# A fused attention and mixture-of-experts kernel: its two hand-written step lists laid in another order

## The chip, the cores and the metric

The kernel runs on one core of a Trainium2 chip. The metric is the device time of one launch in microseconds (us). Engines are named as in the profile: PE (TensorE), PEld (its weight loads), DVE (VectorE), ACT (ScalarE), POOL (GpSimd) and SP, whose queue issues most DMAs.

## The reference

Attention with rotary embedding over 8 batches of 8 heads, 576 tokens, head size 64; its output, 4608 tokens of 512 values, goes to the one of 8 experts with the highest gate logit.

```python
q_rot, k_rot = rotate(q), rotate(k)
scores = scale * q_rot @ k_rot^T            # per batch and head, 576 x 576
attn = exp(scores - max) / (sum + 1e-9)
x = (attn @ v) as [4608, 512]               # heads side by side
expert = argmax(x @ w_gate);  g = softmax weight of that expert
out[token] = g * (relu(x[token] @ w1[expert]) @ w2[expert])
```

## The kernel before

**Two halves.** The attention handles 32 pairs of heads (4 pairs make a batch). The experts follow: tokens are gathered by expert into slots of 256, and each slot does two products (lines 1378 and 1514). The attention's output goes to DRAM (x_dram) batch by batch, and the positions of the tokens are scattered into per-expert lists in DRAM (xlist).

**Steps and their names.** The attention is cut into 2213 small steps. A step is written as a name whose last letter is its engine (p PE, v DVE, a ACT, g POOL, d SP's queue), with the number n of its pair. For a pair:

- FP loads q and k (1152 KB; two buffers, so pair n + 2 waits until pair n is rotated). RKm and RQm multiply by the rotation (POOL), RBb adds the two halves. HB rounds to the high part (ACT), LB makes the low part (POOL), and DX and DY (SP) copy these parts to the other half of the partitions; DW and DZ are small copies of the same kind.
- S0 to S8 are nine score products on PE (lines 760 and 771), each into a pair of PSUM banks; M0 to M8 take the row maxima (DVE), E0 to E8 the exponentials (ACT), which give the banks back.
- TA0, TA1, TB0, TB1 and TR turn the exponentials on PE (lines 798, 831, 835). The ten steps cA0x to cRy copy the results from PSUM to SBUF, on DVE or ACT (line 716); c3 is a small one for the rest rows.
- V0 and V1 are the long products with the values (line 870), V4 is that of the rest rows. U0 and U1 copy their results out, on DVE or ACT (line 897). O turns them back, X scales them into the rows of x (DVE).

Four PSUM pairs are handed round in the order in which the steps take and give them.

**The gate.** After each fourth pair the steps gL to gY find the expert of every token. gP counts on PE; gD, gQ, gO, gU and gY are small steps on POOL; gS stores the rows. gI0 to gI4 are the list scatters: five indirect DMAs a batch that POOL issues (line 1088). Their number is that of the batch's last pair, so gI3 with 23 belongs to batch 5. Those of the last two batches come after the lists.

**What sets the order.** FIRST and LAST name every attention step in the order in which it is emitted. chained_emit ties each instruction to the one before it on its engine, so each engine works in list order; an engine that waits holds up all that stands behind it. A third list, PLAN, gives the places that remain and is not changed.

**The seam.** LAST also holds steps that begin with m: mRI loads the lists of the first three slots (line 556; it needs the last scatter of batch 5), mGA and mGB gather rows of the first two slots (POOL, line 608), mXA and mXB turn them on PE (line 1326), mS.. and mZ.. split the weights in a high part (ACT) and a low part (DVE or POOL, line 1573), and mM1 is the first expert product.

```python
def listed_steps(steps):
    for tok, n in steps:
        if tok[0] == "m":
            chained_emit(lambda: tail[tok[1:-1]](tok[-1]), True)
        elif tok[0] == "g":
            gate_step(tok, n // NP, True)
        else:
            step(tok, n, True)
```

Of the kernel before, what the change touches and what calls it, by code (L numbers as in the profile page):

```python
# [31 lines left out]
    ("RQav", 0), ("RQcv", 0), ("RQbv", 0), ("FPd", 1), ("RKcv", 0), ("HQa", 0), ("RKav", 0), ("DWd", 0), ("DXd", 0),  # L32
    ("LQv", 0), ("RKbv", 0), ("HKa", 0), ("DYd", 0), ("RQcv", 1), ("S4p", 0), ("RQav", 1), ("LKv", 0), ("S3p", 0),
    ("S7p", 0), ("RQbv", 1), ("HQa", 1), ("RKcv", 1), ("M4v", 0), ("M3v", 0), ("E3a", 0), ("LQg", 1), ("FPd", 2),
# [10 lines left out]
    ("DYd", 2), ("M4v", 2), ("TRp", 1), ("E4a", 2), ("cRya", 1), ("cRxv", 1), ("DXd", 2), ("TA0p", 1), ("TB1p", 1),  # L45
# [7 lines left out]
    ("TRp", 2), ("E4a", 3), ("DYd", 3), ("S7p", 3), ("VPd", 2), ("CTd", 0), ("cRyv", 2), ("cA0xa", 2), ("RQmg", 5),  # L53
# [13 lines left out]
    ("TRp", 4), ("VPd", 4), ("FPd", 8), ("LBg", 6), ("VPd", 5), ("cB1xv", 4), ("cA0xv", 4), ("cRxv", 4), ("cA0ya", 4),  # L67
# [1689 lines left out]
```

## Time and profile before

| what | us |
|---|---|
| median of 3 runs (lowest, highest) | 922.22 (920.4, 926.88) |
| the profiled execution | 923.04 |
| its span, first to last instruction | 921.2 |
| PE busy in the span | 903.7 |
| start, up to the first score product | 13.7 |
| attention, 13.7 to 453.9 | 440.2 |
| experts, 453.9 to 921.2 | 467.3 |

The profile is of one execution. A busy PE is one with at least one product in flight; products overlap, so stretched ones count as busy as well.

### The profile page before, as it was taken

What the parts mean: (1) busy time and instruction counts of PE and PEld (TensorE: products, weight loads), DVE (VectorE), ACT (ScalarE), POOL (GpSimd) and SP (SyncE); (2) the same over time, 40 slices, a digit from 0 to 9 for tenths busy, and PEclk for the clock granted to TensorE, in tenths of its full rate; (3) what the DMA queues carried; (4) which work ended last, traced back from release to release, by engine and by line L of the source; (5) the groups of instructions that cost most, each with busy time, mean ns of one, the idle gap of its engine ahead of it and who ended that gap; (6) DMA issues with size and microseconds to landing.
All of it is one profiled execution on the core that took longest, in us unless ns stands there. A gap on an engine that the chain in (4) does not pass through costs nothing.

```text
span 921.2 us, 26711 instructions
## 1 busy us (share of the span) xinstructions
PE 903.7 (98%) x10101; PEld 730.9 (79%) x10101; DVE 748.4 (81%) x1361; ACT 629.1 (68%) x1190; POOL 640.8 (70%) x446
## 2 busy tenths in 40 slices
PE   8999999999999999999999999999999999999997
PEld 7666677677767766766799999999999999997786
DVE  6877788898988978788777677777777777778997
ACT  5888888778878888886645555555555555556886
POOL 3999787898998998894645566666666666664111
PEclk9999999999999999999999999999999999999999
DMA  8677565656674676535521577425426311165991
GB/s 284 185 208 225 158 170 182 216 161 181 198 218 127 184 217 195 158 76 169 204 90 38 146 236 240 125 67 161 125 60 194 97 49 49 44 195 203 406 339 52
DMA packets 71162, 152.73 MB, mean 166 GB/s; under 512 B 28601, under 2 KB 39673, under 8 KB 66032
## 3 DMA queue, kind: packets, MB, share of 16 engines
q1 hardware_dynamic: 61424, 130.69, 45.7%
q0 software_dynamic: 9600, 20.23, 7.0%
q8 instruction: 83, 1.36, 0.6%
q14 instruction: 55, 0.45, 0.2%
HBM read 161.32 MB, written 22.69 MB: 200 GB/s over the span
## 4 chain that ended last, share of the span: by engine, by line
PE 26%; issue 21%; POOL 18%; ACT 2%; POOLq 1%; DMA 1%; DVE 1%; DVEq 0%; ACTq 0%
PE pb L870 6%; POOL xg L589 6%; POOL xt L589 6%; PE pb L1378 5%; PE pb L771 5%; POOL out_dram L1404 4%; PE pb L1514 4%; PE pb L798 3%; POOL xsm L1256 1%; DMA out_dram<-y,gi 1%; PE pb L884 1%; POOLq L1447 1%; PE pb L920 1%; ACT PT L716 1%; ACT pn L787 1%
## 5 line engine op out<-in xcount | busy, mean ns | idle before, releaser
L776 DVE TENSOR_REDUCE negm<-pb 128x1 f32<-128x576 f32 x288 | 205.7, 749 | 45.0 <-PE pb L771 31.1
L787 ACT ACTIVATE pn<-pb,negm 128x576 f32<-128x576 f32 x256 | 188.2, 742 | 56.6 <-DVE negm L776 53.6
L1378 PE MATMUL pb<-xh,w1h 128*128 128x256 f32 x544 | 153.8, 283 | 0.0
L1378 PE MATMUL pb<-xh,w1l 128*128 128x256 f32 x544 | 153.7, 283 | 0.0
L1378 PE MATMUL pb<-xl,w1h 128*128 128x256 f32 x544 | 153.7, 283 | 0.0
L771 PE MATMUL pb<-rKQ 64*128 64x288 f32 x768 | 138.2, 312 | 2.6 <-ACT pn L787 1.0
L771 PE MATMUL pb<-rKQ,rX 64*128 64x288 f32 x768 | 138.4, 312 | 1.3 <-ACT PT L716 0.5
L870 PE MATMUL pb<-PT,vn 128*64 128x320 f32 (+1 forms) x1024 | 138.1, 412 | 0.1
L589 POOL DMA_INDIRECT xg<-x_dram,gp x64 | 91.4, 1428 | 54.6 <-DVE gp L399 38.1
L1282 DVE TENSOR_TENSOR w2l<-r,w2h 128x1024 fp32r<-128x1024 f32 x89 | 107.3, 1216 | 19.6 <-ACT w2h L1281 17.3
L771 PEld LDWEIGHTS pb<-rKQ,rX 64*128 64x128 f32 x768 | 107.5, 185 | 18.6 <-ACT pn L787 7.5
L771 PEld LDWEIGHTS pb<-rKQ 64*128 64x128 f32 x768 | 107.4, 185 | 18.3 <-ACT pn L787 11.1
L589 POOL DMA_INDIRECT xt<-x_dram,gp x56 | 80.4, 1436 | 49.2 <-DVE gp L399 31.7
L716 DVE COPY PT<-pb 128x512 f32<-128x512 f32 (+1 forms) x192 | 100.8, 564 | 11.2 <-PE pb L835 5.7
L870 PEld LDWEIGHTS pb<-PT,vn 128*64 128x64 f32 x1024 | 67.9, 136 | 51.2 <-issue 8.1
L1282 DVE TENSOR_TENSOR w1l<-r,w1h 128x1024 fp32r<-128x1024 f32 x88 | 104.6, 1219 | 2.7 <-ACT w1h L1281 2.2
L1378 PEld LDWEIGHTS pb<-xh,w1h 128*128 128x128 f32 x544 | 106.1, 195 | 0.6
L1378 PEld LDWEIGHTS pb<-xh,w1l 128*128 128x128 f32 x544 | 106.1, 195 | 0.5
L1514 PE MATMUL pb<-w2h,hh 128*128 128x512 f32 x272 | 106.2, 390 | 0.0
L1378 PEld LDWEIGHTS pb<-xl,w1h 128*128 128x128 f32 x544 | 106.1, 195 | 0.0
L1514 PE MATMUL pb<-w2l,hh 128*128 128x512 f32 x272 | 106.0, 390 | 0.0
L1514 PE MATMUL pb<-w2h,hl 128*128 128x512 f32 x272 | 105.9, 389 | 0.0
(224 smaller groups left out, 2014.5 us busy)
## 6 DMA issues: line engine op xcount, KB each, us to landing
r<-in_moe_w_dram SPq DMA_DIRECT2D x136, 512.0 KB
qk<-in_qk_dram SPq DMA_DIRECT2D x31, 1152.0 KB
r<-in_moe_w1q_dram SPq DMA_DIRECT2D x56, 512.0 KB
rX<-rKQ SPq DMA_DIRECT2D x128, 144.0 KB
x_dram<-xt SPq DMA_DIRECT2D x8, 1032.0 KB
vn<-in_v_dram SPq DMA_DIRECT2D x32, 256.0 KB
xlist<-mark SPq DMA_DIRECT2D x3, 408.0 KB
qk<-in_qk_dram SPq DMA_DIRECT2D x2, 576.0 KB
```

Of the source, the lines that this page charges most:

```text
L589: nc.gpsimd.indirect_dma_start(out=t[:, k], out_offset=None, in_=x_dram.rearrange("n (q w) -> (n q) w", q=4), in_offset=bass.IndirectOffse ...
L716: return (nc.scalar.copy if eng == "a" else nc.vector.tensor_copy)(out=o, in_=i).ins
L771: nc.tensor.matmul(sp[:, r, 0:HS], lhsT=(st["KQ"][rows[r], 1] if r == h else st["X"][rows[r]])[:, a, i * P:(i + 1) * P], rhs=parts(st["KQ" ...
L776: nc.vector.tensor_reduce(out=st["negm"][:, j:j + 1], in_=st["S", j][:, :, 0:HS], axis=AX.XY, op=ALU.max, negate=True)
L787: nc.scalar.activation(out=parts(pt), in_=sp[:, :, 0:HS], func=AF.Exp, bias=st["negm"][:, j:j + 1], scale=1.0, accum_out=z)
L798: nc.tensor.transpose(tp[:, r, k * 256 + i * 64:k * 256 + i * 64 + 64], pn[rows[r], i, c:c + P], ident[rows[r], rows[r]])
L870: m = nc.tensor.matmul(st["av"][rows[h ^ half], half, 0:w], lhsT=st["vn"][:, h, kt, :], rhs=st["PT"][:, 4 * h + kt, half * 256:half * 256 ...
L884: m = nc.tensor.matmul(st["av"][rows[h ^ a], a, 0:k * D].rearrange("p (i q) -> p i q", i=k), lhsT=vr[n % NVR][rows[h]], rhs=st["PT"][rows[ ...
L1282: nc.vector.tensor_tensor(out=lo, in0=src, in1=hi.bitcast(F32), op=ALU.subtract)
L1378: m = nc.tensor.matmul(hp[:, fi], lhsT=w, rhs=x, start=(i == 0), stop=(i == len(todo) - 1))
L1404: sc = nc.gpsimd.indirect_dma_start(out=out, out_offset=bass.IndirectOffsetOnAxis(ap=si[:, t:t + 1], axis=0), in_=y, in_offset=None, bound ...
L1514: m = nc.tensor.matmul(yp[:, t], lhsT=h[:, fi, ts_], rhs=w[:, fi], start=(g == 0 and fi == 0 and i == 0), stop=(g == FQ - 1 and fi == 1 an ...
```

## The change

FIRST and LAST are replaced. The new lists hold the same 2213 steps, FIRST 1862 of them and LAST 351 (before: 1845 and 368). Nearly all stand in another place, 90 on another engine: copies out of PSUM (cA0x to cRy) go 29 times from DVE to ACT and 25 times back, U0 and U1 18 times to ACT and 12 times to DVE, c3 three times each way, and mS1l goes from DVE to POOL. The list scatters gI stand at other places among the long products V0 and V1. PLAN and all functions stay. The diff, cut to places that the text speaks of:

```diff
--- before.py
+++ after.py
@@ -29,277 +29,276 @@
     ("gBv", 0), ("gGv", 3),
 ]
 FIRST = [
...
-    ("RQmg", 16), ("E0a", 13), ("S8p", 13), ("RZv", 11), ("M5v", 13), ("E5a", 13), ("Op", 10), ("RKmg", 16),
...
-    ("U0a", 11), ("HBa", 15), ("M2v", 13), ("M6v", 13), ("V1p", 11), ("DXd", 14), ("gYg", 7), ("gI3g", 3),
...
+    ("M6v", 12), ("S2p", 12), ("S1p", 12), ("E6a", 12), ("DXd", 13), ("V1p", 10), ("S4p", 13), ("M1v", 12),
+    ("RKmg", 16), ("HBa", 14), ("E1a", 12), ("TB0p", 12), ("M2v", 12), ("RZv", 11), ("E2a", 12), ("cB0ya", 12),
...
+    ("M6v", 14), ("M1v", 14), ("DXd", 15), ("RQmg", 17), ("S2p", 14), ("gLv", 11), ("gI3g", 3), ("HBa", 16),
...
-    ("V1p", 29), ("E7a", 31), ("E6a", 31), ("mRId", 0), ("U1v", 29), ("S8p", 31), ("mL10d", 0), ("gOg", 27),
-    ("S2p", 31), ("E5a", 31), ("S3p", 31), ("U0v", 29), ("M8v", 31), ("V0p", 30), ("M2v", 31), ("VPd", 31),
-    ("E8a", 31), ("TB1p", 31), ("E2a", 31), ("DZd", 31), ("gSd", 27), ("M3v", 31), ("E3a", 31), ("TRp", 31),
-    ("TB0p", 31), ("cB1ya", 31), ("cRya", 31), ("V4p", 30), ("cRxv", 31), ("cB1xv", 31), ("cB0xv", 31), ("cB0ya", 31),
-    ("Op", 29), ("TA0p", 31), ("mS0ha", 0), ("TA1p", 31), ("cA1ya", 31), ("cA0xv", 31), ("V1p", 30), ("U0a", 30),
-    ("mGAg", 0), ("mS0lg", 0), ("cA0yv", 31), ("cA1xa", 31), ("V0p", 31), ("mGBg", 0), ("gPp", 27), ("mS2ha", 0),
-    ("mS1ha", 0), ("RZv", 31), ("mS3ha", 0), ("Xv", 29), ("mCMx", 0), ("c3v", 31), ("mS1lv", 0), ("gRv", 27),
...
+    ("S8p", 31), ("E6a", 31), ("gOg", 27), ("M8v", 31), ("S2p", 31), ("U1a", 29), ("S3p", 31), ("V0p", 30),
+    ("mS3ha", 0), ("mL10d", 0), ("VPd", 31), ("E8a", 31), ("M2v", 31), ("gI3g", 23), ("M3v", 31), ("mS3lv", 0),
+    ("E2a", 31), ("TB1p", 31), ("E3a", 31), ("cB1yv", 31), ("TB0p", 31), ("cB0ya", 31), ("gSd", 27), ("TA0p", 31),
+    ("cB1xv", 31), ("cB0xa", 31), ("V4p", 30), ("TA1p", 31), ("cA0yv", 31), ("cA0xv", 31), ("mS2ha", 0), ("U0v", 30),
+    ("TRp", 31), ("cA1ya", 31), ("V1p", 30), ("cRxv", 31), ("mS0ha", 0), ("mRId", 0), ("DZd", 31), ("cRya", 31),
+    ("RZv", 30), ("cA1xv", 31), ("mGAg", 0), ("V0p", 31), ("mS0lg", 0), ("mCMx", 0), ("Op", 29), ("c3a", 31),
+    ("mXAp", 0), ("mGBg", 0), ("U1v", 30), ("mL20d", 0), ("V4p", 31), ("gPp", 27), ("mS1ha", 0), ("mX1ha", 0),
+    ("gRv", 27), ("mX0ha", 0), ("mL21d", 0), ("V1p", 31), ("mX1lv", 0), ("mL23d", 0), ("U0a", 31), ("mS2lg", 0),
+    ("mS1lg", 0), ("Op", 30), ("mL22d", 0), ("RZv", 31), ("gUg", 27), ("mZ0ha", 0), ("U1v", 31), ("mX0lv", 0),
+    ("gVv", 27), ("Op", 31), ("gYg", 27), ("mCRx", 0), ("mXBp", 0), ("Xv", 31), ("Xv", 29), ("mM1p", 0), ("Xv", 30),
+    ("mZ3ha", 0), ("mH1ha", 0), ("mH1lv", 0), ("mM0p", 0), ("mM2p", 0), ("mZ3lv", 0), ("mZ2ha", 0), ("mH0ha", 0),
+    ("mH2ha", 0), ("mZ1ha", 0), ("mZ0lg", 0), ("mM3p", 0), ("mZ2lv", 0), ("mY0ha", 0), ("mH0lv", 0), ("mH2lv", 0),
+    ("mN0p", 0), ("mY1ha", 0), ("mLBd", 0), ("mT2ha", 0), ("mT1ha", 0), ("mZ1lv", 0), ("mT0ha", 0), ("mY0lv", 0),
+    ("mY1lv", 0), ("mH3ha", 0), ("mT3ha", 0), ("mN1p", 0), ("mT2lv", 0), ("mN2p", 0), ("mT1lv", 0), ("mT0lv", 0),
+    ("mT3lv", 0), ("mH3lv", 0), ("mN3p", 0), ("mO1a", 0), ("mO0v", 0), ("mLCd", 0),
 ]
```

## Rows read from the trace of the kernel before

**Rows 1.** The page's first part: busy us (share of span) xinstructions by engine.
```profile
PE 903.7 (98%) x10101; PEld 730.9 (79%) x10101; DVE 748.4 (81%) x1361; ACT 629.1 (68%) x1190; POOL 640.8 (70%) x446
```

**Rows 2.** Windows: width, busy us (instructions) by engine, PE's granted clock, DMA share, GB/s.
```profile
13.70:80.00 66.30, 61.31 (x968) 43.78 (x966) 53.60 (x91) 57.86 (x138) 61.05 (x25) 1.00 0.73 216
80.00:200.00 120.00, 118.92 (x1943) 84.07 (x1942) 100.01 (x194) 99.53 (x235) 101.64 (x57) 1.00 0.63 188
200.00:320.00 120.00, 119.40 (x1984) 84.86 (x1982) 107.69 (x214) 94.66 (x222) 110.12 (x64) 1.00 0.60 177
320.00:453.90 133.90, 132.04 (x2184) 92.08 (x2184) 107.39 (x213) 106.87 (x249) 105.47 (x96) 1.00 0.56 168
453.90:921.20 467.30, 459.40 (x2842) 413.56 (x2842) 372.06 (x641) 264.51 (x341) 260.90 (x192) 1.00 0.45 147
```

**Rows 3.** The chain that ended last, in mid-span: start us, us, what.
```profile
287.02 2.30 PE pb L870 x16
300.20 2.31 PE pb L870 x16
```

**Rows 4.** Waits before 454 us: engine, tile <- releaser: us in total, times, longest.
```profile
PEld pb L771 <- ACT pn L787: 18.6, 48, 0.6
POOL qk L710 <- DMA qk<-in_qk_dram: 1.8, 2, 1.0
```

**Rows 5.** Copies of DVE and ACT before 460 us: busy us, mean ns.
```profile
L716 DVE COPY PT<-pb 128x512 f32<-128x512 f32 x144 | 90.4, 680 | 10.6 <-PE pb L835 5.7 <-PE pb L798 4.6 <-ACT pn L787 0.2
L716 ACT COPY PT<-pb 128x512 f32<-128x512 f32 x176 | 93.2, 605 | 7.2 <-PE pb L798 5.9 <-PE pb L835 0.6
```

**Rows 6.** Groups of POOL before 454 us, the list scatters.
```profile
L1088 POOL DMA_INDIRECT xlist<-tid,lpi x30 | 30.6, 1019 | 7.2 <-issue 6.1 <-POOL y L705 0.2
```

**Rows 7.** Timeline of DVE and POOL at 264 us, of DVE at 304 us.
```profile
263.58 3.07 DVE L716 COPY PT<-pb 128x512 f32<-128x512 f32 x5
...
265.74 1.01 POOL L1088 DMA_INDIRECT xlist<-tid,lpi  x1 [0.16 <-issue]
...
303.96 3.07 DVE L716 COPY PT<-pb 128x512 f32<-128x512 f32 x5
```

**Rows 8.** Timeline of SP's queue and of POOL at 330 to 340 us.
```profile
330.05 5.20 SPq L665 DMA_DIRECT2D qk<-in_qk_dram  x2
...
337.30 2.65 POOL L710 TENSOR_TENSOR qk<-qk,rotk 128x1152 f32<-128x1152 f32 x1 [0.98 <-DMA qk<-in_qk_dram]
```

**Rows 9.** Timeline of POOL, SP's queue and PE from 425 to 455 us.
```profile
425.77 1.06 POOL L1088 DMA_INDIRECT xlist<-tid,lpi  x1 [0.46 <-issue]
435.38 0.25 POOL L1058 TENSOR_TENSOR de<-eq,bs 128x40 f32<-128x40 f32 x1 [8.55 <-DVE bs L1055]
436.57 1.15 POOL L608 DMA_INDIRECT xg<-x_dram,gi  x1 [0.54 <-issue]
438.03 1.00 POOL L608 DMA_INDIRECT xg<-x_dram,gi  x1 [0.30 <-issue]
...
431.17 2.73 SPq L556 DMA_DIRECT2D gi<-xlist  x3
...
449.08 0.85 PEld L1326 LDWEIGHTS pb<-cst,xg 128*128 128x128 f32 x8 [0.49 <-issue]
...
454.68 0.37 PE L1378 MATMUL pb<-xh,w1h 128*128 128x256 f32 x1
```

**Rows 10.** DMA issues: out<-in queue xcount, KB each or us to landing.
```profile
x_dram<-xt SPq DMA_DIRECT2D x8, 1032.0 KB
xg<-x_dram,gi POOLq DMA_INDIRECT x4, 5.3
```

**Rows 11.** Timeline of DVE and POOL at 447 to 453 us.
```profile
447.40 1.23 DVE L1573 TENSOR_TENSOR w1l<-r,w1h 128x1024 fp32r<-128x1024 f32 x1 [0.94 <-ACT w1h L716]
449.37 3.29 DVE L1573 TENSOR_TENSOR w1l<-r,w1h 128x1024 fp32r<-128x1024 f32 x1
...
449.22 2.36 POOL L1573 TENSOR_TENSOR w1l<-r,w1h 128x1024 fp32r<-128x1024 f32 x1
```

More of the change, by code (lines that the diff above doesn't have):

```diff
@@ L31 @@
 FIRST = [
-    ("RQav", 0), ("RQcv", 0), ("RQbv", 0), ("FPd", 1), ("RKcv", 0), ("HQa", 0), ("RKav", 0), ("DWd", 0), ("DXd", 0),
-    ("LQv", 0), ("RKbv", 0), ("HKa", 0), ("DYd", 0), ("RQcv", 1), ("S4p", 0), ("RQav", 1), ("LKv", 0), ("S3p", 0),
-    ("S7p", 0), ("RQbv", 1), ("HQa", 1), ("RKcv", 1), ("M4v", 0), ("M3v", 0), ("E3a", 0), ("LQg", 1), ("FPd", 2),
[10 rows of a table removed]
-    ("DYd", 2), ("M4v", 2), ("TRp", 1), ("E4a", 2), ("cRya", 1), ("cRxv", 1), ("DXd", 2), ("TA0p", 1), ("TB1p", 1),
[7 rows of a table removed]
-    ("TRp", 2), ("E4a", 3), ("DYd", 3), ("S7p", 3), ("VPd", 2), ("CTd", 0), ("cRyv", 2), ("cA0xa", 2), ("RQmg", 5),
[13 rows of a table removed]
@@ L67 @@
-    ("TRp", 4), ("VPd", 4), ("FPd", 8), ("LBg", 6), ("VPd", 5), ("cB1xv", 4), ("cA0xv", 4), ("cRxv", 4), ("cA0ya", 4),
[28 rows of a table removed]
-    ("U0v", 6), ("cA1ya", 8), ("Xv", 5), ("gVv", 3), ("TRp", 8), ("S4p", 9), ("RZv", 7), ("cRxa", 8), ("RKmg", 11),
[7 rows of a table removed]
-    ("cA1ya", 9), ("TRp", 9), ("cB1xa", 9), ("DZd", 9), ("DWd", 11), ("E4a", 10), ("RQmg", 12), ("gSd", 3),
[5 rows of a table removed]
-    ("V4p", 8), ("U0v", 8), ("RZv", 8), ("V1p", 8), ("S4p", 11), ("LBg", 11), ("DYd", 11), ("DZd", 10), ("HBa", 12),
[26 rows of a table removed]
-    ("FPd", 17), ("DYd", 14), ("DWd", 15), ("LBg", 15), ("cA1yv", 13), ("cA0xa", 13), ("cRxa", 13), ("TB1p", 13),
[4 rows of a table removed]
@@ L142 @@
-    ("DXd", 15), ("M2v", 14), ("HBa", 16), ("RQmg", 17), ("E2a", 14), ("DYd", 15), ("V1p", 12), ("gMv", 11),
[8 rows of a table removed]
-    ("S1p", 15), ("M1v", 15), ("RQmg", 18), ("HBa", 17), ("RKmg", 18), ("DXd", 16), ("gVv", 11), ("RZv", 13),
[4 rows of a table removed]
-    ("cB1yv", 15), ("S7p", 16), ("FPd", 19), ("DWd", 18), ("M0v", 16), ("DYd", 17), ("gEa", 11), ("DXd", 17),
[14 rows of a table removed]
-    ("RBbg", 20), ("LBg", 19), ("DWd", 19), ("FPd", 22), ("cRxa", 17), ("gI4g", 3), ("cRyv", 17), ("cA0xv", 17),
[56 rows of a table removed]
-    ("E7a", 24), ("DYd", 25), ("U1a", 22), ("gYg", 19), ("TA1p", 24), ("TRp", 24), ("DZd", 24), ("DXd", 25),
[16 rows of a table removed]
@@ L245 @@
-    ("cB0ya", 26), ("DWd", 28), ("cB1yv", 26), ("cB1xa", 26), ("cRxv", 26), ("FPd", 30), ("RBbg", 29), ("cRya", 26),
[3 rows of a table removed]
-    ("gMv", 23), ("c3v", 26), ("gDg", 23), ("DZd", 26), ("DXd", 28), ("M8v", 27), ("S7p", 27), ("gQg", 23),
[4 rows of a table removed]
+    ("FPd", 1), ("RQav", 0), ("RQcv", 0), ("RQbv", 0), ("RKcv", 0), ("RKav", 0), ("HQa", 0), ("LQv", 0), ("RKbv", 0),
+    ("RQav", 1), ("RQcv", 1), ("HKa", 0), ("LKv", 0), ("RQbv", 1), ("DWd", 0), ("RKcv", 1), ("S4p", 0), ("DXd", 0),
[49 rows of a table added]
+    ("RQmg", 9), ("cA1xa", 6), ("cRya", 6), ("cRxv", 6), ("S7p", 7), ("DWd", 8), ("E8a", 7), ("cB1yv", 6), ("VPd", 6),
[20 rows of a table added]
@@ new lines @@
+    ("cA1ya", 9), ("RKmg", 13), ("RBbg", 12), ("cB1xa", 9), ("E4a", 10), ("TRp", 9), ("cRxa", 9), ("cRyv", 9),
[28 rows of a table added]
+    ("M2v", 13), ("V1p", 11), ("gYg", 3), ("DYd", 14), ("gWv", 7), ("M6v", 13), ("gYg", 7), ("E2a", 13), ("DWd", 14),
[10 rows of a table added]
+    ("cB0yv", 14), ("LBg", 16), ("E4a", 15), ("gBv", 11), ("DZd", 14), ("DYd", 15), ("cB1xa", 14), ("gOg", 11),
[7 rows of a table added]
+    ("S4p", 16), ("RKmg", 18), ("cB0xa", 15), ("VPd", 14), ("LBg", 17), ("RQmg", 18), ("RZv", 14), ("RZv", 15),
[29 rows of a table added]
+    ("gQg", 15), ("DZd", 18), ("E0a", 19), ("gBv", 15), ("DWd", 21), ("M5v", 19), ("E5a", 19), ("gOg", 15),
[11 rows of a table added]
@@ L254 @@
+    ("VPd", 19), ("cB1yv", 20), ("gVv", 15), ("TRp", 20), ("RQmg", 23), ("cB1xa", 20), ("cRya", 20), ("cRxa", 20),
[3 rows of a table added]
+    ("M7v", 21), ("DWd", 22), ("gGv", 15), ("RZv", 20), ("M5v", 21), ("E7a", 21), ("FPd", 25), ("RQmg", 24),
[57 rows of a table added]
 ]
 LAST = [
[46 rows of a table removed]
-    ("mLCd", 0),
[33 rows of a table added]
+    ("TRp", 31), ("cA1ya", 31), ("V1p", 30), ("cRxv", 31), ("mS0ha", 0), ("mRId", 0), ("DZd", 31), ("cRya", 31),
[10 rows of a table added]
 ]
```

482 rows, old and new, of tables (FIRST, LAST) are left out of this document.

## The prediction

> **What bounds the kernel now.** I read the stages first, then TensorE's pace inside one of them, then the waits, and last the hand-over between the two halves. The page says that PE is busy for 903.7 us, 98% of the span [rows 1]; that alone could hide stretched instructions, so the windows come next [rows 2]. They cut the span into the start (13.7 us, up to the first score product), the attention (13.7 to 453.9) and the experts (467.3). In all of their rows the granted clock is 1.00, that is 2.4 GHz. In the attention PE has nothing in flight for 66.30 - 61.31 = 5.0 us in the opening, then 1.1, 0.6 and 1.9 us: 8.6 us in 440.2. POOL is the next fullest engine (61.05 of 66.30 in the opening, 110.12 of 120.00 at 200 to 320), then DVE (107.69 of 120.00). So in the opening POOL, which rotates q and k, feeds PE hand to mouth; afterwards PE is the bound and the others run ahead of it.
>
> How much is hidden in stretched products shows in the pace: two neighbouring V1 products stand 300.20 - 287.02 = 13.18 us apart [rows 3], in a window where PE is idle for 0.6 of 120 us. The 32 pairs at that pace take 32 x 13.18 = 421.8 us, and the attention takes 440.2. **The 18.4 us between them are all that any order of the steps can give**, and they hold things that an order can't remove: the filling of the pipeline in the opening (5.0 us of idleness there), its draining, the small count products of eight gates, and the transposes of the first expert rows. What is left to win I put at 5 to 8 us, an estimate from these two rows and the idle sums. The list of waits agrees: the longest that PE's weight loads have is for exponentials that give a PSUM pair back, 18.6 us over 48 waits of at most 0.6 us, most of it under products still in flight [rows 4].
>
> **The change part by part.** It holds two lists of the same 2213 steps. Counted in the diff: 311 of 578 attention steps of TensorE keep their place in PE's own order, and 90 steps change their engine. PE gets the same products, so the stream of 421.8 us stays. The experts' 467.3 us and the start's 13.7 us aren't in the lists, but for their seam.
>
> *Engines.* Of the copies out of PSUM, 29 go from DVE to ACT and 25 back, so 4 net: DVE loses 4 x 0.680 = 2.7 us and ACT gains 4 x 0.605 = 2.4 us [rows 5]. Of the value copies (do_U) 18 go to ACT and 12 come back; no row for them is needed if I price them at a full copy as an upper bound: 6 x 0.680 = 4.1 us off DVE and 6 x 0.605 = 3.6 us onto ACT. ACT was busy for 57.9 + 99.5 + 94.7 + 106.9 = 359 of 440 us [rows 2], so 6 us more are covered by 81 us in which it waits. On the path: 0. If that cover is gone at single places, PE waits there for a copy, 0.6 us each.
>
> *Scatters.* Thirty list scatters run in the attention, 30.6 us at 1.02 each plus 7.2 us of issue [rows 6]: 37.8 us of POOL, in both kernels. Moving them pays only if one of them delays someone. Beside one at 265.74 to 266.75, DVE copies five PSUM blocks in 3.07 us; five such blocks with ordinary POOL additions beside them take 3.07 us as well [rows 7]. The scatters lie from 194 us on, and there PE is idle for 0.6 + 1.9 us in all. So the part that names the change is worth 0 to -2.5 us; I take -0.5, nearer to nothing, because the equal copies are the nearest row. The Trainium skill speaks against a gain too: its page "SBUF — State Buffer", section "Who interferes with whom", says that VectorE and GpSimd exclude each other only when the VectorE instruction has two SBUF inputs (or runs in a two-port mode), and that TensorE never waits on them. These PSUM copies have none, and the equal 3.07 us agree. By that rule the term is 0.0 and the sum 0.5 us later.
>
> *POOL's own order.* Each pair costs POOL four long operations of some 2.65 us [rows 8]. The new list puts RKm of pair 16 behind RBb of pair 14 with only gU and one RQm between (0.26 + 2.65 = 2.9 us of POOL); in the old list the smallest such distance is 9.3 us (pair 27). The step needs the q/k transfer of pair 16, which can't start until RBb of pair 14 frees one of two buffers. The one transfer whose end POOL waited for in mid-stream was issued at 330.05 and used at 337.30, so 7.25 us [rows 8]. POOL therefore waits 7.25 - 2.9 = 4.3 us, with LB of pair 14 queued behind it, for which the DMAs of the low score parts wait. Cover: LB 14 also needs HB 14 on ACT, which the new list has 15 PE steps behind RBb 14, 15/18 of a pair, 11 us; RKm 16 ends after 7.25 + 2.65 = 9.9 us. So 0; bounds 0 to +4.3 if ACT runs ahead of PE there.
>
> *The seam.* The load of the first lists (mRI) moves from 20 to 9 TensorE steps ahead of the first expert product (mM1), and on SP's queue from ahead of the last value load and of the store gS of batch 6 to behind them. It needs the last scatter, which moves from 26 to 16 TensorE steps ahead of mM1 and now stands behind gO of batch 6 on POOL. Before: last scatter issued at 425.77, index loads at 431.17, first gather (GA) at 436.57 and its second half at 438.03 [rows 9], landing 5.3 us after issue [rows 10], so rows at 443.3; PE turned them at 449.08 and mM1 began at 454.68 [rows 9]. The chain from the scatter to the rows is 17.5 us, with 5.8 us to spare. Ten steps later at 13.18/18 = 0.73 us each is 7.3 us, so about 1.5 us too late: PE's transposes of these rows, and the value products queued behind them, would wait that long. Against it: POOL idles for 8.55 us at that point of the old order [rows 9], so the scatter may go earlier than its place. For it: the index loads now queue behind the 1032 KB of gS [rows 10]. Also mS1l moves from DVE to POOL (2.36 us, the third in a row there), behind GA and GB. Bounds 0 to +5; I take +1.5. The two old DVE subtractions of this kind took 1.23 us alone and 3.29 us beside POOL's [rows 11]. The new order may spare DVE the long one, which frees DVE and not PE, still at the value products then: 0. The same section of the Trainium skill foretells the 3.29, since both operations read two SBUF inputs.
>
> *The opening.* POOL's list differs there only in which of RQm and RKm comes first, and POOL sets the pace; 0, bounds -3 to +3 (5.0 us of idleness, of which more than half is the filling).
>
> **Sum** against the profiled execution: 13.7 + 440.2 + 467.3 = 921.2, and 923.04 with the 1.8 us around the span. -0.5 + 0 + 0 + 1.5 + 0 = +1.0, so 924.0. The profiled execution lies 0.8 us above the median of the three runs (922.22); on that scale 923.2, rounded to **923 us**.
>
> **Rivals.** (1) *The waits do go*: the order was laid anew as a whole, so every stall may be planned away. It would give back the 5 to 8 us above plus half of the opening's idleness: 922.2 - 10 = 912 us. For it: 18.4 us lie above the pace. Against it: most have fixed causes, and the steady stretch is already at 13.18. Chance 0.10. (2) *POOL waits for transfers and then the seam slips*: if a q/k transfer needs 10 us rather than 7.25, because lists, fills and values share the DMA engines, five places of the new list come short (POOL work from RBb to the first rotation of the pair after next: 2.9 us at pair 16, 7.2 at pair 17, 7.8, 7.9 and 7.9 at pairs 7, 6 and 13), 7.1 + 2.8 + 2.2 + 2.1 + 2.1 = 16 us of POOL. POOL's idleness in the attention (80 to 320: 28 of 240 us) takes about half, the rest and the seam's 5 reach PE: 8 + 5 = 13, so 935 us. It decides from a landing above about 8 us. Against it: POOL waited for a transfer for just 1.8 us in two waits [rows 4]. Chance 0.14. (3) *The change doesn't do what it says*: in the lists 9 of 30 scatters stand next to a V0 or V1 product in the old order, and 9 in the new one; so what moved is everything else, a reshuffle of equal quality, at 922 us. Chance 0.16; my forecast, with the seam a little late, has 0.60.
>
> **How the numbers follow.** About 1%, 9.2 us, is what a measurement of this kernel can tell from no change. Forecast and rival 3 lie within it. Rival 1 gives over 1% in some 0.07, rival 2 in some 0.12. Faster 0.07, same 0.81, slower 0.12. The range reaches from 914 (the scatters' -2.5, the opening's -3 and a half of rival 1) to 932 (+4.3 on POOL and +5 at the seam).
>
> **What would show it.** Right: V1 products still about 13.2 us apart in mid-span; scatters with nobody waiting behind them; idleness of PE near 8 to 11 us before mM1; mM1 at 454 to 457. A wait of the transposes on the gather shows the seam, a wait of POOL's rotations on the q/k load near pair 16 the queue. Wrong: mM1 before 448 or after 462, a mid-span pace away from 13.2 by more than 0.2, or a change inside the experts' 467 us, which I hold fixed.

## The result, and the profile after

The changed kernel takes 928.97 us (median of 11 runs, 927.97 to 932.36) against 921.90 for the kernel before beside it (11 runs): ratio 1.008, 95% interval 1.0066 to 1.0095. It is 7 us slower, inside the forecast range (914 to 932) and 6 us above the forecast. The profiled execution took 928.38 us, with a span of 926.5, 5.3 us longer than before.

The page's first part and the windows of the changed kernel, cut at the same places as [rows 1, 2] (its first score product starts at 13.43, its last attention step ends at 458.37):

```profile
PE 906.5 (98%) x10101; PEld 730.6 (79%) x10101; DVE 741.1 (80%) x1350; ACT 633.4 (68%) x1200; POOL 641.4 (69%) x447
```

```profile
13.43:80.00 66.57, 61.45 (x976) 43.83 (x976) 55.59 (x96) 58.92 (x138) 63.04 (x26) 1.00 0.76 222
80.00:200.00 120.00, 118.38 (x1930) 83.42 (x1931) 98.20 (x190) 98.20 (x232) 98.82 (x56) 1.00 0.63 182
200.00:320.00 120.00, 118.52 (x1942) 83.29 (x1941) 101.77 (x202) 97.65 (x228) 108.75 (x64) 1.00 0.63 179
320.00:458.37 138.37, 136.08 (x2227) 94.17 (x2227) 105.90 (x211) 108.91 (x256) 107.96 (x95) 1.00 0.55 164
458.37:926.46 468.09, 459.72 (x2843) 413.62 (x2842) 372.46 (x643) 264.02 (x341) 261.16 (x194) 1.00 0.45 146
```

What to see: the page is as good as unchanged, 98% of PE again. The windows say where to look. The attention takes 444.9 us instead of 440.2, so it holds +4.8 (before rounding); PE's idleness in it grew from 8.6 to 10.5 us, so the other 2.9 are stretched products that count as busy. From the last attention step to the first expert product mM1 it is 2.53 us instead of 0.79, +1.7. The start is 0.3 shorter, and from mM1 to the end it is 0.9 shorter, where the two lists are the same but for a few small steps. Together 5.3.

Where in the attention? The first V1 product of the pairs 11 and 28, in the timeline of PE, after and then before:

```profile
193.28 2.10 PE L869 MATMUL pb<-PT,vn 128*64 128x320 f32 x14
...
425.86 2.37 PE L869 MATMUL pb<-PT,vn 128*64 128x320 f32 x16
```

```profile
193.13 2.10 PE L870 MATMUL pb<-PT,vn 128*64 128x320 f32 x14
...
422.66 2.37 PE L870 MATMUL pb<-PT,vn 128*64 128x320 f32 x16
```

Up to pair 11 the two kernels are level. Then 17 pairs take 232.6 us instead of 229.5, 13.68 each instead of 13.50. There is no single hole, but the loss isn't even either. By the first V1 product of each pair, the changed kernel is 0.4 us late at pair 12, 1.3 at 13, 1.1 at 16, 2.1 at 17, 1.9 at 20, 2.5 at 21, 2.1 at 25 and 3.3 at 26. So it comes in steps, each two or three pairs behind the end of a batch (pairs 11, 15, 19, 23), where the lists hold the steps of the gate. That the gate is the cause isn't shown. The waits between 80 and 448 us name one cause that grew and one that looks like a cause (engine, tile <- releaser: us in total, times, longest), after and then before:

```profile
ACT rKQ L715 <- issue: 13.5, 12, 1.6
...
PEld pb L770 <- ACT PT L715: 5.2, 12, 0.8
...
PEld pb L797 <- ACT PT L715: 2.0, 5, 0.6
```

```profile
ACT rKQ L716 <- issue: 8.0, 7, 1.6
...
PEld pb L771 <- ACT PT L716: 3.1, 7, 1.0
...
PEld pb L798 <- ACT PT L716: 1.1, 2, 0.6
```

Score products and transposes wait longer for copies of ACT out of PSUM (7.2 us against 4.2). My own sum, the time from each PE step's start to the next one's less the lower quartile of such pairs of steps, gives 5.5 against 2.4 us for the steps that an ACT copy ended. And ACT sits idle 5.5 us more ahead of its rounding step HB (the rows with rKQ).

The seam, in the timeline of the changed kernel (POOL, SP's queue, PE's weight loads):

```profile
436.32 1.06 POOL L1087 DMA_INDIRECT xlist<-tid,lpi  x1 [0.40 <-issue]
447.21 1.07 POOL L607 DMA_INDIRECT xg<-x_dram,gi  x1 [9.83 <-DMA gi<-xlist]
448.59 1.00 POOL L607 DMA_INDIRECT xg<-x_dram,gi  x1 [0.30 <-issue]
449.61 2.37 POOL L1572 TENSOR_TENSOR w1l<-r,w1h 128x1024 fp32r<-128x1024 f32 x1
452.14 1.00 POOL L607 DMA_INDIRECT xt<-x_dram,gi  x1 [0.16 <-issue]
453.45 1.01 POOL L607 DMA_INDIRECT xt<-x_dram,gi  x1 [0.30 <-issue]
...
444.28 2.75 SPq L555 DMA_DIRECT2D gi<-xlist  x3
...
458.30 0.14 PEld L1325 LDWEIGHTS pb<-cst,xt 128*128 128x128 f32 x1
459.91 0.74 PEld L1325 LDWEIGHTS pb<-cst,xt 128*128 128x128 f32 x7 [1.47 <-DMA xt<-x_dram,gi]
460.90 0.20 PEld L1377 LDWEIGHTS pb<-xh,w1h 128*128 128x128 f32 x1 [0.25 <-DVE lgt L946]
```

The last scatter now starts at 436.32 (425.77 before, [rows 9]), the index loads at 444.28, the first gather at 447.21, the second at 452.14 and 453.45 behind a subtraction on POOL. PE has turned the first slot's rows without a wait and then stands 1.47 us at the second slot's.

### The profile page after: what moved, and what is told of

Read it like the earlier page. It is cut to its first block, busy times and chain, and to the rows that moved or that the text cites. A ratio compares the mean times of both kernels' runs of the same rounds, so it can differ in the third digit from the quotient of the medians.

```text
span 926.5 us, 26670 instructions
## 1 busy us (share of the span) xinstructions
PE 906.5 (98%) x10101; PEld 730.6 (79%) x10101; DVE 741.1 (80%) x1350; ACT 633.4 (68%) x1200; POOL 641.4 (69%) x447
## 4 chain that ended last, share of the span: by engine, by line
PE 42%; issue 23%; POOL 19%; ACT 7%; DMA 6%; DVE 2%; POOLq 1%; SPq 0%; DVEq 0%; ACTq 0%
PE pb L869 11%; PE pb L770 9%; POOL xt L588 6%; POOL xg L588 6%; PE pb L797 5%; PE pb L1377 5%; POOL out_dram L1403 4%; PE pb L1513 4%; ACT pn L786 3%; ACT PT L715 2%; PE pb L883 2%; PE pb L919 2%; PE pb L759 1%; POOL xsm L1255 1%; DMA out_dram<-y,gi 1%
## 5 line engine op out<-in xcount | busy, mean ns | idle before, releaser
L715 ACT COPY PT<-pb 128x512 f32<-128x512 f32 (+1 forms) x196 | 99.3, 572 | 12.7 <-PE pb L797 6.7
```

What stands on the lines that cost most here:

```text
L715: return (nc.scalar.copy if eng == "a" else nc.vector.tensor_copy)(out=o, in_=i).ins
```

## The experiments

There were twelve runs, on three chips, called B, C and D here (A is the chip of the result). The changed kernel itself ran on A, C and D, but not on B. On B, C and D the kernel before takes 930 to 931 us, 8 to 9 more than on A, so ratios to before on the same chip are compared; the us in the expectations of e1 to e4 are those of A. A step that is moved into the other list stands there behind the same number of PE steps, as far as the list allows. "Attention" and "seam" (last attention step to mM1) come from each run's one trace.

| run | edit | chip | us | before | ratio (95%) | attention | seam |
|---|---|---|---|---|---|---|---|
| result | the change | A | 928.97 | 921.90 | 1.0080 (1.0066 to 1.0095) | 444.9 | 2.53 |
| e1 | after, old engines | B | 948.69 | 931.24 | 1.0201 (1.0183 to 1.0219) | 465.6 | 1.50 |
| e4 | before, new engines | B | 945.29 | 931.24 | 1.0168 (1.0151 to 1.0185) | 459.9 | 0.77 |
| e3 | before, scatters part of the way to new places | B | 934.67 | 931.24 | 1.0056 (1.0036 to 1.0076) | 451.9 | 0.78 |
| e2 | after, early last scatter | B | 936.18 | 931.24 | 1.0053 (1.0040 to 1.0066) | 454.7 | 1.49 |
| b0 | before again | C | 929.83 | 930.27 | 1.0000 (0.9981 to 1.0019) | 446.6 | 0.78 |
| a0 | after again | C | 934.48 | 930.27 | 1.0031 (1.0015 to 1.0048) | 448.4 | 4.99 |
| e5 | after, old scatter places | C | 939.85 | 930.27 | 1.0096 (1.0074 to 1.0118) | 453.5 | 4.07 |
| e8 | after, HB later | C | 937.33 | 930.27 | 1.0069 (1.0049 to 1.0090) | 452.3 | 2.02 |
| a1 | after again | D | 932.89 | 930.23 | 1.0028 (1.0014 to 1.0043) | 449.8 | 1.50 |
| f1 | after, early second gather | D | 933.00 | 930.23 | 1.0019 (1.0004 to 1.0035) | 450.8 | 1.49 |
| f2 | after, 7 copies from ACT to DVE | D | 935.84 | 930.23 | 1.0058 (1.0036 to 1.0081) | 450.7 | 1.14 |
| f3 | f1 and f2 | D | 935.23 | 930.23 | 1.0040 (1.0024 to 1.0055) | 452.2 | 1.14 |

**Engines without order, order without engines: e1 and e4.** The 90 places are copies; mS1l, the one other step that changes its engine, stays as its list has it. One of the 90 places of e1 (e4 does the reverse in the old list):

```diff
-("cRya", 15)   # after
+("cRyv", 15)   # as in the old list
-("U1a", 16)
+("U1v", 16)
```

> The changed kernel with the 90 copies back on the engines of the old lists (every other order as in the changed kernel; PE, POOL and SP issue the same sequences as after). Theory A, the copies' new engines cost: between the two traces the stalls of PE that end with a copy of ACT out of PSUM grow from 2.4 to 5.5 us by my sum over the steps, so undoing the 90 gives back some 3 us of the 7: 926 us. Theory B, the new order of the steps itself costs: nothing comes back, 928 to 930 us.

> The kernel before with the 90 copies on the engines of the new lists, order unchanged. Theory A, the new engines cost by themselves: 925 us. Theory B, the new order costs: 922 us, within 1 us of before. If both this one and the changed kernel with the old engines are slow, engines and order were fitted to each other and only fit together.

Neither theory held. The old engines in the new order give 1.0201, against 1.003 for the change on C and D and 1.0080 on A: 1.2 to 1.7% worse, 11 to 16 us. The new engines in the old order cost 1.68%, also 16 us. So the 90 places are worth more than 10 us in either list, and each set only pays with its own order, the case named last in the text on e4. The stalls show it in both: in e1 PE waits for value copies (uT) of DVE, which it did in the changed kernel once for 0.5 us and in the kernel before not at all, and in e4 for DVE's copies out of PSUM, up to 2.4 us at a time. Waits of e1 from 80 to 480 us, then of e4 from 80 to 475:

```profile
PEld pb L797 <- DVE uT L896: 1.1, 2, 0.7
...
PEld pb L869 <- DVE uT L896: 0.8, 1, 0.8
```

```profile
PEld pb L771 <- DVE PT L716: 4.5, 5, 2.4
...
PE pb L771 <- DVE PT L716: 3.1, 3, 2.2
```

These rows are a part of the loss. In the attention PE has nothing in flight for 24.1 us in e1 and 20.9 in e4, against 12.2 in a0 and 11.0 in b0; most of the difference isn't assigned to single steps.

**The scatters alone: e3 and e5.** e3 moves them part of the way in the old list: counted in PE steps it goes 156 of the 407 steps that the change moves the 30 scatters, and 10 stay where they were. e5 puts all 30 back in the new list. For one of them:

```diff
 # e3, in the old list
-("V4p", 26), ("S0p", 28), ("gI3g", 19), ("gI3g", 15), ("DZd", 28),
+("gDg", 23), ("DZd", 26), ("gI3g", 19), ("DXd", 28), ("M8v", 27),
 # e5, in the new list
-("FPd", 30), ("V4p", 24), ("gI3g", 19), ("RBbg", 29), ("HBa", 28),
+("Xv", 25), ("S2p", 28), ("gI3g", 19), ("gI3g", 15), ("DYd", 29),
```

> The kernel before with its 30 list scatters alone at the places (counted in TensorE steps) that the new lists give them. My prediction's term for the scatters is -0.5 us with bounds 0 to -2.5; at the seam the last scatter now stands 10 steps later while the index load keeps its place, which can add up to 1.5. Theory A, the scatters matter to nobody but the seam: 921 to 924 us. Theory B, their places among the long products are where the loss of 7 us comes from (POOL's rotations behind them come late): 926 us or more. Theory C, they help: 919 us or less.

> The changed kernel with its 30 list scatters at the places (counted in TensorE steps) of the old lists, all else unchanged. The scatters' new places, put half way into the old lists, gave 1.0056 in place of 1. Theory A, the places of the scatters hold the loss: 0.4 to 0.8% come back, ratio about 1.002. Theory B, the loss is in the order of the other steps, and a scatter belongs where its own list puts it: nothing comes back or it gets slower, ratio 1.008 to 1.014.

e3 is 0.56% or 5 us worse than before, theory B's size; its interval reaches from 0.36 to 0.76%, and of its eight executions five take 933 to 935 us and three 938 to 939. e5 is 1.0096 against 1.0031 of a0 beside it, 6 us worse, as theory B said. So taking scatters out of their own list's places costs some 5 us in either direction, and their new places are not the loss. How a scatter reaches PE stays open: the low parts that POOL makes are done 4 to 17 us ahead of the first score product of their pair in all four traces (b0, e3, a0, e5; at the least 4.4 in b0 and 5.2 in e3). So late rotations, the way named in the text on e3, aren't seen.

**The early scatter: e2.**

```diff
-("gEa", 27), ("gI0g", 23), ("gBv", 27),
-("M2v", 31), ("gI3g", 23), ("M3v", 31),
+("TB0p", 30), ("gI0g", 23), ("gI3g", 23), ("gDg", 27),
-("mS0ha", 0), ("mRId", 0), ("DZd", 31),
+("mL10d", 0), ("mRId", 0), ("VPd", 31),
```

> The changed kernel with the last two list scatters of batch 5 (gI0 and gI3) ahead of gD of batch 6 and the first index load (mRI) right behind mL10, as in the old lists; nothing else moved. Theory A, the seam: PE's second transpose of expert rows waits 1.3 us for the second gather, and 1.6 us pass between its first and its second product; with the scatter some 5 us earlier this wait goes and the time falls by 1.3 to 1.7 us, to about 927.4. Rival: the gather of the second slot is held by POOL's 2.4-us subtraction ahead of it and not by the lists: then its issue stays at 452 to 453 us and the time at 929.

Theory A's wait did go (the second slot's rows are turned from 468.26 without one), but not by an earlier gather. What the rival named holds: POOL stands before the subtraction, and the gather behind it starts later than in any trace of the change (452.14 on A, 456.47 in a0, 455.27 in a1):

```profile
457.49 2.36 POOL L1572 TENSOR_TENSOR w1l<-r,w1h 128x1024 fp32r<-128x1024 f32 x1 [7.72 <-ACT w1h L715]
459.99 1.02 POOL L607 DMA_INDIRECT xt<-x_dram,gi  x1
```

It is no wait because the attention ends later still. Whether the time fell can't be said: 1.0053 lies between 1.003 on C and D and 1.0080 on A. Windows of e2 around the place where the scatters now stand, and its weight loads at 437 us and at mM1:

```profile
438.00:441.00 3.00, 1.99 (x31) 1.62 (x30) 0.78 (x2) 0.79 (x3) 1.86 (x5) 1.00 1.01 324
441.00:443.00 2.00, 1.65 (x12) 0.85 (x12) 1.93 (x8) 0.74 (x3) 0.56 (x2) 0.60 1.04 382
443.00:445.00 2.00, 2.00 (x12) 0.89 (x8) 0.54 (x2) 1.33 (x4) 0.00 (x0) 0.55 0.21 84
```

```profile
437.67 0.20 PEld L919 LDWEIGHTS pb<-iw,uT 64*64 64x64 f32 x3 [0.53 <-issue]
...
469.82 0.19 PEld L1377 LDWEIGHTS pb<-xh,w1h 128*128 128x128 f32 x1 [0.70 <-DVE lgt L946]
```

From 435 to 440 us PE stops five times for 0.35 to 0.53 us with nothing released, two thirds busy; then the granted clock falls to 0.60 and 0.55 (near 1.2 GHz, where it was 2.4) for some 4 us. From the first V1 product of pair 28 to that of pair 29 e2 takes 17.19 us, against 12.46 in the trace of the result. And mM1 waits 0.70 us for the last X step of DVE (line 946): the new list puts two X steps just ahead of mM1, and these give back the PSUM pair that mM1 takes. In the old list they stand behind it, and mM1 follows the second transposes by 0.86 us, here by 1.56.

**The controls: a0 and b0.**

> The changed kernel, nothing altered, on the chip of the runs beside it: the first four experiments ran on a chip on which the kernel before takes 931 us and not 922, so the changed kernel is wanted there too. Both theories (the loss is a property of the lists; the loss depends on the chip): a ratio of 1.007 to 1.010 to before if it is of the lists; 1.00 or over 1.015 if it depends on the chip.

> The kernel before, nothing altered, for its trace on the chip of the runs beside it. Expected: a ratio of 1.00; if this chip gives 931 us too, 8 to 9 us more than the first trace, I expect them in the attention from 200 us on (the experts' products take 372.3 us in all traces so far) and as stalls of PE at single steps, not as a slower pace of all.

Neither forecast of a0 held: the change costs 0.3% on C and not 0.8. b0 is level with before, as it must be, and as expected the experts take the same time (465.8 against 466.5 us from mM1 to the end) and the extra us lie in the attention: 446.6 against 440.2. By V1 products b0 is no later than the first trace until pair 17, 0.2 us late at pair 21 and 6.0 at pair 27. Part of it is stops of PE in the middle of a step, with no releaser: five of 0.4 to 0.6 us between 200 and 402 us in b0, one in the whole attention of the first trace. One of them:

```profile
329.60 0.19 PEld L920 LDWEIGHTS pb<-iw,uT 64*64 64x64 f32 x3 [0.15 <-issue]
330.35 0.28 PEld L920 LDWEIGHTS pb<-iw,uT 64*64 64x64 f32 x9 [0.56 <-issue]
```

The largest part is one place. From the first V1 product of pair 26 to that of pair 27 the old order takes 14.45 us on A, but 18.16 in b0, and 17.34 and 17.36 in e3 and e4 on B. In b0 PE stops there, and then its granted clock falls to 0.50, which is 1.2 GHz. Weight loads of b0 and its windows (columns as in [rows 2]):

```profile
402.88 0.18 PEld L771 LDWEIGHTS pb<-rKQ,rX 64*128 64x128 f32 x1 [0.67 <-issue]
...
405.54 0.33 PEld L771 LDWEIGHTS pb<-rKQ,rX 64*128 64x128 f32 x1
```

```profile
403.00:406.00 3.00, 2.44 (x30) 2.09 (x32) 2.31 (x6) 2.61 (x7) 2.84 (x2) 0.78 0.01 3
406.00:408.00 2.00, 2.00 (x38) 1.87 (x40) 1.92 (x4) 1.66 (x5) 1.98 (x2) 0.50 0.50 114
```

The new order takes 14.44 us for these pairs on A, 14.95 in a0 and 14.97 in a1. So at pair 26 the changed kernel is 2.7 us late on C (3.3 on A), and one pair later 0.5 us early. In these traces the smaller ratio on C is a loss of the old order on that chip rather than a smaller cost of the change. Whether that is so in every execution isn't shown: the five of 23 on C in which the kernel before kept a mean clock of 0.999 or more take 929.6 to 931.3 us, hardly less than the median of all, 930.3.

In a0 the attention is 1.8 us longer than in b0 (4.8 on A), but the seam costs 5 us, since the second gather is later still:

```profile
462.03 0.14 PEld L1325 LDWEIGHTS pb<-cst,xt 128*128 128x128 f32 x1
465.68 1.36 PEld L1325 LDWEIGHTS pb<-cst,xt 128*128 128x128 f32 x7 [3.51 <-DMA xt<-x_dram,gi]
```

**HB later: e8.** One of 24 moves, past exponentials only:

```diff
-("V1p", 16), ("HBa", 20), ("M6v", 18), ("E1a", 18), ("M2v", 18), ("S4p", 19), ("RZv", 16), ("E6a", 18),
+("V1p", 16), ("M6v", 18), ("E1a", 18), ("M2v", 18), ("S4p", 19), ("RZv", 16), ("E6a", 18), ("HBa", 20),
```

> The changed kernel with ACT's rounding step HB of 14 pairs moved behind one or two exponentials, so that at most one exponential of the pair two before it is still to come (24 moves by 1 to 7 places, all else unchanged). HB overwrites the buffer of pair n - 2 and so waits for that pair's last score product; where three exponentials were still queued behind it, ACT sat idle for 1.2 us before it. ACT's idleness before HB sums to 10.3 us in the old trace and 15.8 in the new one. Theory A, these 5.5 us reach PE, since the exponentials behind HB give the PSUM pairs back: 2 to 4 us come back, ratio 1.004 to 1.006. Theory B, they are hidden by products in flight: within 1 us of the changed kernel.

ACT's wait ahead of HB is gone as designed (13.3 us in a0), in the view of waits from 80 to 448 us, but others came:

```profile
ACT pn L786 <- DVE negm L775: 59.8, 71, 2.7
POOL rKQ L728 <- ACT rKQ L715: 17.4, 10, 2.9
...
PEld pb L797 <- ACT rKQ L715: 2.6, 6, 0.4
...
ACT rKQ L715 <- issue: 1.5, 2, 0.8
```

The kernel is 1.0069 against 1.0031, 3.5 us slower. Theory A falls, and theory B's "within 1 us" as well. ACT is not less idle for it: ahead of its exponentials it now waits 59.8 us for DVE's maxima (40.9 in a0), and from 80 to 448 us it is idle for 73.6 us (69.8 in a0). What waits for HB waits longer: POOL's low part 17.4 us (6.5 in a0) and PE's transposes 2.6 us (0.4). So the wait ahead of HB was not what PE lost; that these two waits are the 3.5 us isn't shown.

**The seam and the bursts: a1, f1, f2, f3.**

```diff
 # f1
-("mGAg", 0), ("V0p", 31), ("mS0lg", 0), ("mCMx", 0), ("Op", 29), ("c3a", 31), ("mXAp", 0), ("mGBg", 0),
+("mGAg", 0), ("mGBg", 0), ("V0p", 31), ("mS0lg", 0), ("mCMx", 0), ("Op", 29), ("c3a", 31), ("mXAp", 0),
 # f2, one of seven
-("cRxa", 29)
+("cRxv", 29)
```

> The changed kernel, nothing altered, as the control of the three runs beside it. On two chips it gave 1.008 and 1.0031 of before, so I expect a ratio between the two, and PE's wait for the second gather (1.3 us on one, 3.5 us on the other) between these as well.

> The changed kernel with the second gather (mGB) directly behind the first (mGA) on POOL, ahead of the subtraction mS0l, which waits for ACT; all else unchanged. Theory A, PE's wait at the seam is for a gather that stands behind that subtraction: the gather starts 2.5 us earlier or more, the wait (1.3 to 3.5 us) goes, the first expert product comes 1 to 1.5 us after the last step of the attention and no longer 2.5 to 5 us, and the ratio falls by 0.0015 to 0.004 against the control. Rival, POOL's three subtractions behind it then set the start of the first product: the wait goes over to them and the ratio stays.

> The changed kernel with 7 copies out of PSUM moved from ACT to DVE (cRy of pair 7, cB0x of 9, cRx of 14, 22, 26 and 29, cB1y of 27): each is the copy whose end let PE go on after a stall of 0.3 to 0.9 us, and each stood at the end of three to five ACT copies in a row. Theory A, these bursts of ACT copies are what the new order loses in the attention: the 7 stalls sum to 2.8 us, of which 1.5 to 2.8 us come back, ratio 0.0015 to 0.003 below the control. Theory B, copies and order are fitted to each other, and DVE's maxima behind the moved copies then come late: ratio at the control or above it.

> Both edits of the two runs beside it. If the seam and the bursts are independent losses, the ratio is the control's less both of theirs (0.003 to 0.007 lower, so 0.998 to 1.004); if the time won in the attention only moves the wait to the seam, less than that.

a1 repeats a0's ratio (1.0028, so not between the two chips' as forecast), and in its trace PE did not wait for the second gather at all. That wait is 1.5, 3.5 and 0 us in the three traces of the change and is not the steady part of the loss. f1 starts the gather as wanted, but the ratio stays within the intervals (1.0019 against 1.0028; with f2's edit in both, f3 against f2, 1.0040 against 1.0058). In its trace the seam is as long as a1's, because the 0.7 us for the X step remain:

```profile
451.85 1.00 POOL L607 DMA_INDIRECT xt<-x_dram,gi  x1 [0.30 <-issue]
453.15 1.00 POOL L607 DMA_INDIRECT xt<-x_dram,gi  x1 [0.31 <-issue]
...
466.82 0.19 PEld L1377 LDWEIGHTS pb<-xh,w1h 128*128 128x128 f32 x1 [0.71 <-DVE lgt L946]
```

f2 is 0.3% worse than the control (1.0058 against 1.0028, with intervals that just overlap), as theory B said: taking the seven copies that ended PE's waits from ACT gains nothing. That they make DVE's other work late isn't shown. f3 lies between f1 and f2, as two independent edits would, but the intervals can't tell more. No edit beats the kernel before; f1 is the nearest.

## Why the prediction was right in its range, and where a step failed

**The bound and the scale.** Right in the main: PE's stream is unchanged, neighbouring V1 products in mid-span still stand some 13.2 us apart (13.38 between 288.67 and 302.05, where [rows 3] had 13.18), the experts keep their time, and PE's idleness of 10.5 us in the attention is within 8 to 11. mM1 at 460.90 is past the 454 to 457 that I called right and short of the 462 that I called wrong. Two neighbours are not the mean: from pair 11 to 28 the kernel before already takes 13.50 us a pair, so less of the 18.4 us was open to an order than the one distance says. The measured 0.8% is within the 1% that I took for no change. That the range held is in part luck: its upper end was made of 4.3 us on POOL and 5 at the seam. POOL gave 0 and the seam 1.7, and the 4.8 us of the attention came from parts that I had put at nothing.

**Engines, "on the path: 0".** This step failed, and with it the silent term beside it, that a reshuffle of PE's own order costs nothing. I took the 90 copies as net counts (4 copies out of PSUM, 6 value copies) and covered them by 81 us in which ACT waits. e1 and e4 show that neither net counts nor idle sums tell the cost: e4 makes the same net move in the old list, against the same idle sum, and loses 16 us, and e1 makes the reverse of it in the new list and loses 11 to 16. My condition, "if that cover is gone at single places", is the one that came, and 0.6 us each was short of it, since single stalls in e4 reach 2.4 us. In the change both parts come together and cancel but for the 4.8 us that the attention loses on A (1.8 in the traces of C, where the old order loses 3.7 us more than on A at pair 26). The loss in steps from pair 12 on comes with a PE that waits longer for ACT's copies, 7.2 against 4.2 us in the two rows on A and 8.0 against 4.3 on C. That these waits cause it was argued from the trace, and the one test of it (f2) gained nothing. So the terms for engines and order, 0 together, are mis-sized: +4.8 on A. At which steps it is lost stays open.

**Scatters, -0.5 with bounds 0 to -2.5.** That they give next to nothing was right: e5 shows that undoing their move in the new list gains nothing. But the bounds were not bounds of moving them alone, which costs some 5 us (e3, e5). The equal copies beside a scatter [rows 7] say that a scatter does not slow DVE; they say nothing of what is queued behind it.

**POOL's order, 4.3 us of waiting and 0 on the path.** Right in its size and its effect. The timeline of POOL in the changed kernel at RKm of pair 16, whose transfer SP issued at 173.62:

```profile
173.76 2.65 POOL L709 TENSOR_TENSOR qk<-qk,rotq 128x1152 f32<-128x1152 f32 x1
180.29 2.64 POOL L709 TENSOR_TENSOR qk<-qk,rotk 128x1152 f32<-128x1152 f32 x1 [3.88 <-DMA rX<-rKQ]
```

POOL stands for 3.88 us (the profile names another DMA of that moment as the releaser, so that the transfer ended the wait is my reading; it had been on its way for 6.67 us), and the two kernels are level at pair 11's V1 13 us later.

**The seam, +1.5 with bounds 0 to +5.** +1.7 on A, and 0.7 to 4.2 in the other traces of the change: the size and the bounds held. The mechanism held half: I had the first slot's transposes wait and the value products behind them. They did not; the second slot's did, whose gather stands behind mS0l. And the wait for the PSUM pair behind the X steps (0.25 us on A, 0.7 in a1, e2 and f1) I had not seen in the lists. The long subtraction went as forecast: DVE's stands alone in the new order,

```profile
443.41 1.22 DVE L1572 TENSOR_TENSOR w1l<-r,w1h 128x1024 fp32r<-128x1024 f32 x1
```

where [rows 11] had one of 3.29 us beside POOL's. This agrees with the Trainium skill, page "SBUF — State Buffer", section "Who interferes with whom", on a VectorE operation with two SBUF inputs beside a GpSimd operation that reads SBUF. The seam is no shorter for it.

**The rivals.** The waits did not all go (rival 1). Rival 2's queue for transfers appeared at pair 16 without harm. Rival 3, a reshuffle of equal quality, is nearest to C and D: 0.3% apart.

## What to carry to other kernels

A hand-laid order and its engine assignment are one object: each half of this change alone costs 1.7 to 2.0%, both together 0.3 to 0.8%. So don't price a move of many steps by net counts and idle sums; look instead at each moved step for who gets a buffer back from it. An engine that idles, even just ahead of a step that others wait for, is not proof of a loss: e8 took 12 us of such waiting away, they came back ahead of other steps, and the kernel was slower. And where two kernels are less than 1% apart, compare them on more than one chip.

## What the runs showed of the hardware

The same two programs compare differently on different chips: 1.0080 on A, 1.0031 and 1.0028 on C and D, with the kernel before 1% slower there. The extra time lies in the attention: from mM1 to the end every trace takes 465.5 to 466.5 us. Part of it is the stops of PE in the middle of a step, which recur at the same place of PE's stream: counted in loads, products and waits from the start, at number 13,861, 13,859 and 13,861 in a0, e2 and f1, which share that order, and at 10,541, 10,537 and 10,540 in b0, e3 and e4, which share the other. They go with the program's place and not with the moment (e1 has the first of them at 449.24 us, a0 at 435.42), but not with the place alone: on A, and in e5, PE passes the same place without a stop. Busy DMA queues are no condition: the DMA share in the 2 us ahead of the stops was anything from 0.03 to 1.13. The Trainium skill, page "Runtime: NRT & Kernel Launch", section "Instruction fetch mechanics", says that an engine's instructions are refilled in blocks by a DMA queue of its own and that the cost is mostly hidden. The page of the profile counts such transfers (packets, MB, share), without saying for which engine:

```profile
q8 instruction: 83, 1.36, 0.6%
```

In a0's trace one of them is under way from 434.07 to 435.34 us, just ahead of a0's stop at 435.42. But on A one is under way at the same place (431.45 to 432.58) and PE doesn't stop, and none is in the 1.5 us ahead of the stop at 330.35 in b0. So that this is the cause stays open.

After some such stops, or a long wait, the granted clock fell to about 1.2 GHz for some us, and weight loads and products were stretched (a load of line 771 takes 0.33 us in b0 at 405.54 and 0.18 at 402.88): the clock was 0.55 of full speed in e2 after PE had been busy 1.99 of 3 us, 0.50 in b0 (the windows above), and 0.69 as a mean over 3 us in a0 right after the 3.5 us at the second gather. It does not follow every stop: a1 has a stop at the same place as a0 and stays at full speed to the end of the attention.
